# Decay and phase sums of a gated recurrence per chunk, in 64-row tiles of TensorE

## The chip, the cores and the metric

One Trainium2 chip, one core. The metric is the device time of one execution in microseconds; shown are the median and the range of the runs. PE is TensorE, DVE is VectorE, ACT is ScalarE, POOL is GpSimd, SP is SyncE.

## What is computed

A linear recurrence with a complex decay over 768 steps, for 4 batches of 8 heads of width 48, and then a layer norm and a two-layer network with a residual. Cut to what matters:

```python
mag = sqrt(a_re**2 + a_im**2); scale = minimum(mag, 0.999) / (mag + 1e-6)
ar, ai = a_re * scale, a_im * scale
for t in range(768):
    S_re, S_im = ar[t] * S_re - ai[t] * S_im + outer(k[t], v[t]), ar[t] * S_im + ai[t] * S_re
    y[t] = q[t] @ S_re
x = y with the heads side by side            # 4 x 768 x 384
xn = (x - mean) / sqrt(var + 1e-6) * g_ln
out = x + maximum(xn @ w_ch1, 0) @ w_ch2     # 384 -> 1536 -> 384
```

## The kernel before, in words

Time is cut into chunks of 128 steps, and two neighbouring chunks make a pair (P = 0 to 11, three for each batch; C = 128, R = 2). The recurrence is computed in the usual chunked way. For each pair the logarithm of the decay's magnitude (tile `l`) and its angle (`th`) are worked out, and both are summed over time. With `e = exp(sum)` and `en = exp(-sum)`, `ke = k * en` and `qe = q * e`; with cosine and sine of the summed angle (`trig`) these become `ks` and `qs`, in which the cosine and the sine part of a head lie side by side (48 of 64 columns each). Within a chunk n, scores `am` = ksT and qsT multiplied, masked into `atm`, times v; from earlier chunks comes the state `G`, times qsT. The sum of both is `y`, copied to `x`.

The tiles `l` and `th` hold two time steps in each of 128 partitions: partition p has steps 2p and 2p + 1 of the pair. So chunk 0 of a pair lies in partitions 0 to 63, chunk 1 in 64 to 127. The sum over time is done by TensorE: for each chunk c and step j a matmul with a matrix of zeros and ones (`u_e`, and `u_th` scaled to turns), four matmuls of 384 columns for the decay (`dec`, line 477) and four for the phase (`ph`, line 496). The kernel before sums over the whole pair: chunk 1 sees all 128 partitions. Two more matmuls of each phase sum (line 492) add, through the matrix `pick`, a constant and the phase carried over from the pair before (tile `car`, rows 96 to 127). `car` is copied out of the phase sum's bank after each pair (lines 504 to 512), the phase being read as a 16-bit integer, which takes it modulo one turn.

The state is kept relative to the start of a pair. For chunk 0 the products `ks` times v are added to the old state, which an identity matmul brings into the bank (line 641), and the result is copied to `G` without scaling. Chunk 1's products are added in the same bank, and there the state is scaled by the decay of the whole pair (`G`, line 658). That decay is the last row of `e`, turned onto partitions by eight one-column matmuls (`dps`, line 573) and copied into `dec` (`decc`, line 583).

Then each chunk's x is transposed (`xtr`, `xT`), and the network runs on the pair: `mm1` (line 722), `relu`, `mm2` (line 754), and `ot`, which applies the norm's scale and adds x. The norm's gain and mean are folded into the first weights (`wp`, `wc`).

The order of the work is written out by hand as a plan: a text of tokens `name:engine` with the PSUM bank, and each engine takes its tokens in that order. A token with `@other` waits in addition for that other operation. DMA issues are tokens too: most on SP, some on ACT, the weights on POOL. `warm` tokens are matmuls without use, 256 columns wide, that fill PE at the start. Pair 0 is split into two halves of four heads (`PARTS`), and its two chunks share a bank.

Of the kernel before, what the change touches and what calls it, by code (L numbers as in the profile page):

```python
# [9 lines left out]
FP32 = mybir.dt.float32  # L10
# [29 lines left out]
aim.0.0:A tab.log.0:A aim.0.1:A ue:G are.0.0:S are.0.1:S pad.e.1:G uth:V one:G warm.0:P0 pad.ks.0:G warm.1:P0  # L40
warm.2:P0 pick:G warm.3:P0 are.1.0:S warm.4:P0 warm.5:P0 warm.6:P0 k.0.1:S ln.0.0:A warm.7:P0 car0.1:G warm.8:P0
cmean:G iv.0.0:A warm.9:P0 ident:G warm.10:P0 warm.11:P0 r.0.0:V warm.12:P0 warm.13:P0 warm.14:P0 aim.1.0:S warm.15:P0
warm.16:P0 warm.17:P0 ln.0.1:A warm.18:P0 warm.19:P0 r2.0.0:A warm.20:P0 k.0.0:S warm.21:P0 warm.22:P0 warm.23:P0
warm.24:P0 u.0.0:A warm.25:P0 warm.26:P0 warm.27:P0 warm.28:P0 iv.0.1:A warm.29:P0 l.0.0:V warm.30:P0 are.2.0:S
# [12 lines left out]
warm.110:P2 warm.111:P2 warm.112:P2 qe.1.0.0:V warm.113:P2 warm.114:P2 pad.qs.1:G warm.115:P2 warm.116:P2 l.2.0:V
th.0.0:A warm.117:P2 warm.118:P2 wl.2:G warm.119:P2 ph.0.0:P1 th.0.1:A th.1.0:A qe.0.0.0:V ph.0.1:P4 qe.0.1.0:V
warm.120:P0 warm.121:P0 warm.122:P0 k.1.0:S car.0.0:V1 decc.0:V5 sin.0.0:A1 lc.2.0:V sin.0.1:A4 qt.0.0:P1 ks.0.0.1:V
warm.123:P0 car.0.1:A4 wgc:V cos.0.0:A1 qt.0.1:P4 ph.1.0:P6 k.1.1:S ks.0.1.1:V cos.0.1:A4 qs.0.1.1:V th.2.0:A  # L60
qs.0.0.1:V qs.0.1.0:V wp.1:P5 ks.0.1.0:V sin.1.0:A6 qs.0.0.0:V ks.0.0.0:V qT.1:P4 wc.1.2:V5 tab.log.2:A qT.0:P1
qsT.1:V4 kT.1:P0 qs.1.0.1:G@wc.1.2 dec.2.0:P2 car.1.0:V6 ln.3.0:A warm.124:P4 qsT.0:V1 warm.125:P4 wp.0:P4 e.2.0:A2
are.4.0:S wc.1.0:V5 kT.0:P1 en.2.0:A2 vf.1.0:S ksT.1:V0 ksT.0:A1 wc.0.0:V4 vf.1.1:S am.1:P2 warm.126:P0 wc.1.1:V5
iv.3.0:A warm.127:P0 am.0:P0 wc.0.2:V4 qt.1.0:P6 tab.trig.3:A warm.128:P5 warm.129:P5 warm.130:P5 warm.131:P5
wc.0.1:V4 warm.132:P5 warm.133:P5 atm.0:V0 ph.2.0:P4 r.3.0:G@wc.0.1 cos.1.0:A6 k.2.0:S v.0:A wp.2:P6 atm.1:V2
aim.4.0:S sin.2.0:A4 gm.0:P7 ke.1.0.0:G y.0:P0 G.0:V7 k.2.1:S x.0:A0 qt.2.0:P4 ke.1.0.1:V gm.1:P7 cos.2.0:A4 y.1:P1
q.2.0:S qs.1.0.0:V xtr.0:P0 ks.1.0.0:V x.1:A1 qT.2:P3 th.3.0:A ks.1.0.1:V qT.3:P5 qsT.2:V3 xtr.1:P1 q.2.1:S xT.0:A0
r2.3.0:G@ks.1.0.1 kT.3:P4 qsT.3:A5 xT.1:V1 kT.2:P2 ksT.3:V4 mm1.0.0.0:P0 G.1:V7 q.3.1:S tab.log.4:A v.1:G am.3:P4
ksT.2:V2 mm1.0.0.1:P0 are.5.0:S ke.2.0.0:G atm.3:V4 ln.4.0:A mm1.0.1.0:P2 q.3.0:S wl.3:G mm1.0.1.1:P2 relu.0.0:A0
wc.2.0:V6 am.2:P4 wc.2.2:V6 relu.0.1:A2 gm.2:P7 k.3.0:S atm.2:V4 ph.3.0:P0 qe.2.0.0:G@wc.2.2 G.2:A7 k.3.1:S iv.4.0:A  # L70
y.3:P2 wl.4:G wc.2.1:V6 y.2:P3 x.3:A2 gm.3:P7 pad.ks.2:G u.3.0:A mm1.0.2.0:P4 x.2:V3 r.4.0:G@wc.2.1 bn.3:V xtr.2:P6
xtr.3:P3 mm1.0.2.1:P4 xT.2:A6 xT.3:V3 G.3:V7 tab.trig.5:A mm1.1.1.0:P2 relu.0.2:V4 qe.2.0.1:G are.6.0:S mm1.1.1.1:P2
sin.3.0:A0 wl.5:G mm1.1.2.1:P6 bn.0:V vf.2.0:S relu.1.1:A2 mm1.1.0.1:P4 pad.qs.2:G l.3.0:V mm1.1.2.0:P6 abs.3.0:A0
r2.4.0:V mm1.1.0.0:P4 th.4.0:A car.3.0:V0 mm2.0.0:P2 relu.1.0:A4 ke.2.0.1:V mm2.1.0:P3 qs.2.0.1:V vf.2.1:S cos.3.0:A
lc.3.0:V mm2.2.0:P4 qs.2.0.0:V bn.2:V tab.log.6:A qT.4:P5 mm2.1.1:P3 bn.1:V rstd.1:G dec.3.0:P0 ks.2.0.1:V u.4.0:A
ks.2.0.0:V mm2.0.1:P2 rstd.0:G en.3.0:A0 l.4.0:V ksT.5:S mm2.2.1:P4 e.3.0:A0 lc.4.0:V ln.5.0:A relu.1.2:V6
qe.3.0.1:G@lc.4.0 mm2.1.2:P3 qe.3.0.0:G mm2.0.2:P2 aim.5.0:S oa.1:A3 qT.5:P0 iv.5.0:A vf.3.0:A ot.0:V2 dec.4.0:P6
qsT.4:V5 mm2.2.2:P4 e.4.0:A6 vf.3.1:A qs.3.0.1:V kT.4:P1 qs.3.0.0:V en.4.0:A6 dps.3:P5 are.7.0:S dps.4:P2 ksT.4:V1
ke.3.0.0:G@qs.3.0.0 qT.6:P3 qsT.5:A0 ph.4.0:P6 ot.2:V4 aim.6.0:S ke.3.0.1:G ln.6.0:A decc.3:V5 decc.4:V2 am.4:P4
q.4.0:S v.2:G qsT.6:V3 mm2.3.0:P1 iv.6.0:A atm.4:V4 ks.3.0.1:G k.4.0:S qT.7:P2 tab.trig.7:A mm2.3.1:P1 qsT.7:V2  # L80
gm.4:P3 am.5:P4 sin.4.0:A6 ks.3.0.0:V k.4.1:S y.4:P2 atm.5:V4 r.5.0:G@ks.3.0.0 kT.6:P0 car.4.0:A6 mm2.3.2:P1 x.4:A2
G.4:A3 ksT.6:V0 k.5.1:S kT.7:P5 abs.4.0:A6 xtr.4:P4 ot.1:G y.5:P0 ksT.7:V5 q.4.1:S th.5.0:A am.6:P6 x.5:V0 v.3:G
k.5.0:S am.7:P2 xT.4:A4 atm.6:V6 xtr.5:P0 ph.5.0:P4 r2.5.0:G xT.5:A0 cos.4.0:A ot.3:V1 gm.6:P0 mm1.2.1.1:P6 atm.7:V2
G.6:A0 vf.4.1:A r.6.0:G aim.7.0:S abs.5.0:A4 y.6:P1 mm1.2.1.0:P6 x.6:V1 sin.5.0:A4 vf.4.0:A mm1.2.2.1:P2 relu.2.1:V6
cos.5.0:A xtr.6:P1 r2.6.0:G y.7:P4 mm1.2.2.0:P2 th.6.0:A st.0:A x.7:V4 gm.7:P0 bn.7:V xtr.7:P4 tab.log.8:A ke.4.0.1:G
mm1.2.0.0:P6 xT.6:V1 mm1.2.0.1:P6 q.5.1:S xT.7:V4 qe.4.0.0:G G.7:V0 u.5.0:A are.8.0:S mm1.3.0.1:P4 bn.6:V ke.4.0.0:G
# [3 lines left out]
q.6.0:S r.7.0:V mm2.4.0:P1 e.5.0:A4 qT.8:P7 q.7.0:S bn.5:V v.4:A r2.7.0:G@r.7.0 dec.6.0:P4 are.9.0:S bn.4:V  # L90
relu.3.2:A2 mm2.4.1:P1 k.6.0:S qsT.8:V7 mm2.6.1:P0 rstd.2:G en.6.0:A4 qe.5.0.1:V am.8:P2 ke.5.0.0:V e.6.0:A4
mm2.4.2:P1 qe.5.0.0:V ln.8.0:A atm.8:V2 gm.8:P7 ke.5.0.1:G@qe.5.0.0 q.6.1:S am.9:P4 iv.8.0:A mm2.6.2:P0 qe.6.0.0:G
atm.9:V4 u.7.0:A st.1:A mm2.5.2:P6 ph.6.0:P2 G.8:A7 vf.6.0:A ks.5.0.1:V k.6.1:S tab.trig.9:A qs.5.0.1:V mm2.7.0:P4
ot.4:V1 abs.6.0:V2 y.8:P5 th.7.0:A vf.5.1:A mm2.7.1:P4 l.7.0:V x.8:A5 vf.5.0:A gm.9:P7 y.9:P1 sin.6.0:A2 vf.6.1:A
# [119 lines left out]
def kernel(  # L214
# [115 lines left out]
    def c_pick():  # L330
        nc.gpsimd.memset(pick, 0.0)
# [492 lines left out]
```

## Time and profile before

| | |
|---|---|
| median of 3 runs | 191.35 us (191.23 to 193.47) |
| profiled execution | 192.75 us, its span 191.0 us |
| PE busy | 177.3 us (93%) |
| VectorE, ScalarE busy | 156.6 us (82%), 158.9 us (83%) |
| GpSimd busy | 105.5 us (55%) |
| DMA | 37.57 MB, 197 GB/s in the mean |

The page's busy times are sums over the whole span. A stage that is limited by loads and one that is limited by PE are mixed in them, so busy time is also read by stretches. A line of a grouped view gives: line, engine, operation, output and input by the program's names, shapes and count, then busy time, the mean duration of one in ns, and the idle time before with what ended it. A line of the chain of waits or of the timeline starts with the start and the duration in us.

### The profile page before, as it was taken

How to read it: one execution, taken by the hardware profiler on the slowest of the kernel's cores; microseconds unless marked ns; L12 is line 12 of the kernel's file. 1: busy time of each engine (PE TensorE's matmuls, PEld its weight loads, DVE VectorE, ACT ScalarE, POOL GpSimd, SP SyncE). 2: the span in 40 equal slices, each digit the busy share in tenths (PEclk: the TensorE clock that was granted, in tenths of full speed). 3: DMA queues.
4: the chain of work that ended last, by engine and by line, in shares of the span. 5: the costliest groups of instructions: out<-in, count | busy, mean ns of one | idle time of the engine just before them, and what ended most of it. 6: DMA issues, size and time to landing. Idle time of an engine off the chain costs nothing.

```text
span 191.0 us, 5154 instructions
## 1 busy us (share of the span) xinstructions
PE 177.3 (93%) x2045; PEld 138.6 (73%) x2045; DVE 156.6 (82%) x285; ACT 158.9 (83%) x224; POOL 105.5 (55%) x124
## 2 busy tenths in 40 slices
PE   5999398999999999999968999999999999998992
PEld 3888365788667887776847687877867777786781
DVE  1678699999999999999996998998989867666532
ACT  3989499999999997899949999998999979662340
POOL 7419032579196899071539483347785954940130
PEclk9999999999999999999999999999999999999998
DMA  6999999999969999889999999999799979994032
GB/s 153 278 240 202 212 198 204 210 214 207 242 108 287 205 220 234 154 183 234 136 265 234 190 221 230 282 223 204 141 160 262 217 126 179 256 191 151 5 124 82
DMA packets 133080, 37.57 MB, mean 197 GB/s; under 512 B 127168, under 2 KB 133056, under 8 KB 133056
## 3 DMA queue, kind: packets, MB, share of 16 engines
q1 hardware_dynamic: 107760, 27.21, 70.6%
q10 hardware_dynamic: 22512, 7.67, 18.0%
q0 software_dynamic: 2784, 2.36, 7.9%
q8 instruction: 16, 0.26, 0.6%
q14 instruction: 8, 0.07, 0.1%
HBM read 28.31 MB, written 4.72 MB: 173 GB/s over the span
## 4 chain that ended last, share of the span: by engine, by line
PE 63%; DVE 10%; ACT 9%; DMA 8%; issue 4%; ACTq 2%; POOL 1%; SPq 1%; DVEq 0%; POOLq 0%
PE banks L754 22%; PE banks L722 16%; PE banks L617 5%; PE banks L594 4%; DMA q<-in_q_dram 4%; DMA ksT<-ks 3%; PE banks L477 3%; PE banks L667 2%; ACTq L777 2%; PE banks L496 2%; PE banks L670 2%; DVE w1b L388 2%; DMA are<-in_a_re_dram 2%; PE banks L645 2%; PE banks L688 2%
## 5 line engine op out<-in xcount | busy, mean ns | idle before, releaser
L754 PE MATMUL banks<-w2b,h 128*128 128x384 bf16 (+1 forms) x300 | 55.7, 319 | 0.6 <-ACT h L739 0.6
L722 PE MATMUL banks<-xT,w1b 128*128 128x256 bf16 x432 | 50.9, 272 | 0.7 <-ACT h L739 0.5
L722 PEld LDWEIGHTS <-w1b 128*128 128x128 bf16 x432 | 41.4, 98 | 7.0 <-issue 1.2
L754 PEld LDWEIGHTS <-h 128*128 128x128 bf16 x300 | 26.7, 97 | 13.8 <-ACT h L739 1.0
L295 DVE TENSOR_TENSOR atm<-banks,mask 128x1024 bf16<-128x1024 f32 x24 | 29.0, 1219 | 3.8 <-PE banks L617 2.9
L739 ACT ACTIVATE h<-banks 128x1024 bf16<-128x1024 f32 (+1 forms) x26 | 25.7, 1009 | 4.6 <-DVE ks L295 2.6
L792 ACT ACT_TABLE_LOAD x19 | 24.4, 1283 | 2.6 <-PEq L808 1.3
L295 POOL TENSOR_TENSOR ke<-k,en 128x384 bf16<-128x384 f32 x17 | 15.4, 916 | 14.1 <-ACT e L481 4.3
L767 POOL TENSOR_TENSOR ot<-ot,x 128x384 f32<-128x384 f32 x13 | 12.5, 967 | 14.2 <-ACT ot L760 12.9
L295 POOL TENSOR_TENSOR r<-aim,are 128x768 f16<-128x768 f32 (+1 forms) x8 | 13.7, 1715 | 11.0 <-DVE w1b L388 4.1
L787 PE MATMUL banks<-u_e 128*128 128x256 f16 x134 | 17.5, 286 | 2.2 <-POOL u_e L323 2.2
L295 POOL TENSOR_TENSOR qs<-qe,trig 128x768 bf16<-128x768 bf16 x8 | 13.0, 1640 | 10.3 <-DVE w1b L388 7.2
L617 PE MATMUL banks<-qsT,ksT 128*128 128x128 bf16 x192 | 14.5, 219 | 2.8 <-ACT h L739 2.1
L787 PEld LDWEIGHTS <-u_e 128*128 128x128 f16 x134 | 13.5, 102 | 4.5 <-POOL u_e L323 1.9
L617 PEld LDWEIGHTS <-ksT 128*128 128x128 bf16 x192 | 12.1, 97 | 5.1 <-issue 2.8
L741 DVE TENSOR_SCALAR h<-banks 128x1024 bf16<-128x1024 f32 (+1 forms) x11 | 12.7, 1166 | 2.7 <-PE banks L722 2.7
L295 POOL TENSOR_TENSOR qe<-q,e 128x384 bf16<-128x384 f32 x12 | 11.0, 917 | 6.8 <-DVE r L295 3.6
L466 DVE SCALAR_TENSOR_TENSOR l<-r,w 128x768 f16<-128x768 f16 (+1 forms) x13 | 12.6, 969 | 1.3 <-ACT r L462 1.1
L680 DVE BATCH_NORM_STATS2 stats<-x 128x6 f32<-128x384 bf16 x24 | 13.1, 546 | 0.1
L667 PE MATMUL banks<-v,atm 128*128 128x48 bf16 x192 | 12.0, 183 | 0.0
L514 ACT ACTIVATE trig<-banks 128x768 bf16<-128x768 int16 (+1 forms) x13 | 9.8, 761 | 2.5 <-DVE car L509 2.4
L496 PE MATMUL banks<-th,u_th 128*128 128x384 f16 (+1 forms) x52 | 11.8, 313 | 0.0
(93 smaller groups left out, 380.8 us busy)
## 6 DMA issues: line engine op xcount, KB each, us to landing
k<-in_k_dram SPq DMA_DIRECT2D x24, 192.0 KB, 5.1
q<-in_q_dram SPq DMA_DIRECT2D x24, 192.0 KB, 4.3
are<-in_a_re_dram SPq DMA_DIRECT2D x11, 384.0 KB, 5.1
aim<-in_a_im_dram SPq DMA_DIRECT2D x11, 384.0 KB, 5.0
out_dram<-ot ACTq DMA_DIRECT2D x19, 192.0 KB, 3.4
vf<-in_v_dram ACTq DMA_DIRECT2D x18, 192.0 KB, 4.3
w1b<-in_moe_w_ch_dram POOLq DMA_DIRECT2D x3, 384.0 KB, 7.6
vf<-in_v_dram SPq DMA_DIRECT2D x6, 192.0 KB, 7.0
```

The lines of the kernel that those rows point to most:

```text
L295: {"DVE": nc.vector, "POOL": nc.gpsimd}[eng(name)].tensor_tensor(**kw)
L466: nc.vector.scalar_tensor_tensor(out=S_("l"), in0=S_("r2"), scalar=0.5, in1=S_("w"), op0=ALU.mult, op1=ALU.add)
L496: nc.tensor.matmul(heads(ps[:, c]), lhsT=u_th[:, c, j], rhs=step(T("th", P), j), start=False, stop=(j == R - 1), skip_group_check=True)
L617: nc.tensor.matmul(ps[:, h], lhsT=T("ksT", n)[:, h], rhs=T("qsT", n)[:, h], start=True, stop=True)
L667: nc.tensor.matmul(ps[:, h], lhsT=T("atm", n)[:, h], rhs=T("v", P)[:, c, h], start=True, stop=nfirst)
L680: nc.vector.bn_stats(out=T("stats", n), in_=T("x", n))
L722: nc.tensor.matmul(ps[:, jj], lhsT=w1b[:, dc, ts(gi * JG + jj, C)], rhs=T("xT", P)[:, dc].rearrange("p c t -> p (c t)"), start=(dc == 0), ...
L739: act(out=dst, in_=src, func=AF.Relu)
L741: nc.vector.tensor_scalar(out=dst, in0=src, scalar1=0.0, scalar2=None, op0=ALU.max)
L754: nc.tensor.matmul(bank(own)[:, 0:w], lhsT=T("h", P)[:, j, ts(c, C)], rhs=w2b[:, j, es], start=(j == 0), stop=(j == NJ - 1))
L787: g.add(f"warm.{i}", lambda i=i: nc.tensor.matmul(bank(f"warm.{i}")[:, 0:256], lhsT=u_e[:, 0, 0], rhs=u_e[:, 1].rearrange("p j t -> p (j t ...
L792: g.add(f"tab.{nm}.{i}", lambda tab=tab: nc.scalar.preload_act_table_set(tab))
```

## The change

- Decay sums: for pairs 1 to 11 the matmul of chunk c takes only the rows of its chunk (64 partitions) of `u_e` and of `l`, in the order c = 0, c = 1 for each j. Pair 0 keeps full rows, with the part of `u_e` that joins chunk 1 to chunk 0 set to zero.
- Phase sums: the same for pairs 1 to 11. The carry is added to chunk 0 by one matmul with 64 rows. A new step `car1` copies the phase at the end of chunk 0 to rows 96 to 127 of `car`, and a new matmul `ph2` adds it to chunk 1. The carry to the next pair now lies in rows 32 to 63. Sine, cosine, absolute value and carry wait for `ph2`.
- State: scaled after each chunk, on VectorE. The identity matmul stands in every chunk but the first of a batch, behind the products. `dps` takes the last rows of both chunks, and also runs for the last pair of a batch.
- The plan is another one: other order, other engines for a part of the copies, products and DMA issues, 52 tokens with `@` where there were 27, and 64 fill-ins of 512 columns where there were 134 of 256.

```diff
-        for row in (HALF, C - 1):
+        nc.gpsimd.tensor_copy(out=pick, in_=pick_f)
+        for row in (HALF - 1, C - 1):
...
+    def c_pickf():
+        nc.vector.memset(pick_f, 0.0)
+        for c in range(R):
+            nc.vector.memset(pick_f[ds(c * HALF, 1)], 1.0)
+    def c_uz():
+        nc.vector.memset(u_e[0:HALF, 1], 0.0)
...
-                for c in range(R):
-                    for j in range(R):
-                        nc.tensor.matmul(heads(ps[:, c]), lhsT=u_e[:, c, j], rhs=step(T("l", P), j),
-                                         start=(j == 0), stop=(j == R - 1))
+                for j in range(R):
+                    for c in range(R):
+                        rows = ds(c * HALF, HALF) if NS == 1 else slice(0, C)
+                        nc.tensor.matmul(heads(ps[:, c]), lhsT=u_e[rows, c, j],
+                                         rhs=step(T("l", P), j)[rows],
+                                         start=(j == 0 and (NS == 1 or c == 0)), stop=(j == R - 1),
+                                         skip_group_check=True)
...
+                if NS == 1:
+                    for j in range(R):
+                        for c in range(R):
+                            rows = ds(c * HALF, HALF)
+                            nc.tensor.matmul(heads(ps[:, c]), lhsT=u_th[rows, c, j],
+                                             rhs=step(T("th", P), j)[rows], start=(j == 0),
+                                             stop=False, skip_group_check=True)
+                    nc.tensor.matmul(ps[:, 0], lhsT=(pick_f if first else pick)[lo],
+                                     rhs=T("car", P)[lo, fs], start=False, stop=True,
+                                     skip_group_check=True)
+                    return
...
+                add(f"car1.{X}", lambda X=X, fs=fs, v16=v16: f_car(
+                    f"car1.{X}", T("car", P)[96:C, fs], v16()[96:C, 0]),
+                    needs=[f"ph.{X}", f"car0.{P % RINGS['car']}"], uses=[("car", P)], ps=(f"ph.{X}", nb))
+                add(full, lambda X=X, fs=fs, view=view: nc.tensor.matmul(
+                    view(f"ph.{X}")[:, 1], lhsT=pick[HALF:C], rhs=T("car", P)[HALF:C, fs],
+                    start=False, stop=True, skip_group_check=True),
+                    needs=[f"ph.{X}", f"car1.{X}", "pick"], uses=[("car", P)], ps=(f"ph.{X}", nb))
...
-                needs=[f"ph.{X}"], uses=[("trig", P)], ps=(f"ph.{X}", nb))
+                needs=[full], uses=[("trig", P)], ps=(f"ph.{X}", nb))
...
+        ncol = H if last else R * H
+            for i in range(ncol):
+                nc.tensor.matmul(bank(f"dps.{P}")[:, ds(i, 1)], lhsT=row[:, ds(i * D, C)],
+                                 rhs=ident[:, C - 1:C], start=True, stop=True)
...
+                    for h in range(H):
+                        nc.tensor.matmul(heads(ps)[:, h], lhsT=T("ks", P)[:, c, h],
+                                         rhs=T("v", P)[:, c, h], start=(h == 0), stop=nfirst,
+                                         skip_group_check=True)
+                    if not nfirst:
                         nc.tensor.matmul(ps, lhsT=ident,
                                          rhs=T("G", n - 1).rearrange("p h d -> p (h d)"),
-                                         start=True, stop=True, skip_group_check=True)
+                                         start=False, stop=True, skip_group_check=True)
...
+                add(f"G.{n}", lambda n=n, c=c: tt(
+                    f"G.{n}", out=T("G", n), in0=heads(bank(f"gm.{n}")[:, 0:DM]),
+                    in1=T("dec", P)[:, c].unsqueeze(2).to_broadcast([C, H, D]), op=ALU.mult),
...
-    for i in range(134):
+    for i in range(64):
         g.add(f"warm.{i}", lambda i=i: nc.tensor.matmul(
-            bank(f"warm.{i}")[:, 0:256], lhsT=u_e[:, 0, 0], rhs=u_e[:, 1].rearrange(
-                "p j t -> p (j t)"), start=True, stop=True), needs=["ue"], ps=(f"warm.{i}", 1))
+            bank(f"warm.{i}"), lhsT=u_e[:, 0, 0], rhs=u_th.rearrange(
+                "p c j t -> p (c j t)"), start=True, stop=True), needs=["ue", "uth"], ps=(f"warm.{i}", 1))
```

More of the change, by code (lines that the diff above doesn't have):

```diff
@@ L39 @@
 PLAN = """
[L40 to L44, printed above, removed]
@@ L60 @@
[L60 to L64, printed above, removed]
@@ L70 @@
[L70 to L74, printed above, removed]
@@ L90 @@
[L90 to L94, printed above, removed]
@@ new lines @@
+v.4:G@r.7.0 ln.8.0:A dps.5:P4 decc.5:V4 mm2.6.1:P0 qsT.8:V7 dec.6.0:P4 qe.5.0.1:G en.6.0:A4 e.6.0:A4 iv.8.0:A
+ke.5.0.0:G@r.7.0 bn.5:V mm2.5.1:P6 bn.4:V am.8:P2 atm.8:V2 mm2.4.1:P1 vf.5.1:A am.9:P4 atm.9:V4 k.6.0:S are.9.0:S
+mm2.5.2:P6 ph.6.0:P2 car1.6.0:V2 rstd.3:A rstd.2:A qe.6.0.0:G@r.7.0 gm.8:P7 G.8:V7 u.7.0:A mm2.7.0:P4 ph2.6.0:P2
+qe.5.0.0:G@lc.6.0 ot.5:V6 qs.5.0.1:V vf.5.0:S vf.6.1:A tab.trig.9:A th.7.0:A sin.6.0:A2 l.7.0:V y.8:P5 y.9:P7
+aim.8.0:S x.9:A7 abs.6.0:V2 mm2.7.1:P4 aim.9.0:S mm2.7.2:P4 car.6.0:A2 qs.5.0.0:V mm2.4.2:P1 ot.1:G@qs.5.0.1 oa.7:A4
```

277 lines of the change are left out of this document (138 added, 139 removed).

## The prediction

> **What bounds the kernel now.** I read the page's head and chain first, then busy time by stretch.
>
> ```profile
> span 191.0 us, 5154 instructions
> PE 177.3 (93%) x2045; PEld 138.6 (73%) x2045; DVE 156.6 (82%) x285; ACT 158.9 (83%) x224; POOL 105.5 (55%) x124
> PE 63%; DVE 10%; ACT 9%; DMA 8%; issue 4%; ACTq 2%; POOL 1%; SPq 1%; DVEq 0%; POOLq 0%
> ...
> core 0: us, PE busy (x) PEld busy (x) DVE busy (x) ACT busy (x) POOL busy (x), PEclk, DMA share, GB/s
> 0.00:36.00 36.00, 29.64 (x298) 23.08 (x298) 26.64 (x51) 29.41 (x45) 15.77 (x37) 1.00 1.00 211
> 36.00:187.00 151.00, 147.44 (x1748) 115.50 (x1747) 129.00 (x234) 129.53 (x181) 89.71 (x87) 1.00 0.98 196
> 187.00:191.00 4.00, 0.21 (x3) 0.00 (x0) 0.92 (x3) 0.00 (x0) 0.00 (x0) 0.78 0.29 98
> ```
>
> Three stages. Until about 36 us the fill-in matmuls keep PE busy and loads and ScalarE set the pace. From 36 to 187 us PE is busy 147.44 of 151.00 us at full granted clock, with ScalarE and VectorE near 129, so in this stage a microsecond of matmul work is nearly a microsecond of time. The only slack to win back there is 151.00 - 147.44 = 3.56 us. The last 4 us are the final output and its store. The change reorders those too, but ends as before on a half-width output add and its store, so I give the end nothing.
>
> The profiled execution took 192.75 us for a span of 191.0 (1.75 around it); the three runs have a median of 191.35. I work out a difference and add it to the median. 2% of it, 3.8 us, is about what a measurement of this kernel can tell from no change.
>
> **What PE saves by 64-row tiles.** A matmul's mean is no price, as neighbours overlap; the price is the step from start to start.
>
> ```profile
> L477 PE MATMUL banks<-l,u_e 128*128 128x384 f16 x44 | 8.9, 326 | 0.0
> L641 PE MATMUL banks<-G,ident 128*128 128x384 bf16 x8 | 2.6, 326 | 0.0
> L594 PE MATMUL banks<-ident,ks 128*128 128x128 bf16 x80 | 5.9, 219 | 0.0
> L573 PE MATMUL banks<-ident,e 128*128 128x1 bf16 x64 | 2.5, 164 | 0.1
> ...
> 44.13 0.66 PE banks L722 x6
> 53.04 0.65 PE banks L477 x4
> 58.21 0.45 PE banks L594 x8
> 58.66 0.38 PE banks L573 x16
> ...
> 41.98 0.32 PE L492 MATMUL banks<-car,pick 96*128 96x384 f16 x1
> 42.15 0.49 PE L496 MATMUL banks<-th,u_th 128*128 128x384 f16 x2
> 42.47 0.33 PE L492 MATMUL banks<-car,pick 96*128 96x384 f16 x1
> 42.64 0.49 PE L496 MATMUL banks<-th,u_th 128*128 128x384 f16 x2
> 42.97 0.18 PE L667 MATMUL banks<-v,atm 128*128 128x48 bf16 x1
> ```
>
> Four decay matmuls hold the path for 0.65 us, so one 384-wide matmul costs 0.163; the six of a phase sum run from 41.98 to 42.97, again 0.163 each. The 326 ns mean is twice that: 0.163 of flow, and 0.163 of tail that normally hides under the next matmul.
>
> For eleven of the twelve pairs (pair 0, split in two, keeps whole-row tiles) the four decay matmuls become two couples, rows 0-63 and rows 64-127, in two banks. If a couple runs side by side, four steps become two: 11 x 2 x 0.163 = -3.58 us. The phase sum goes from six steps to two couples, one carry matmul and one more for chunk 1 ("ph2"), four in all: again 11 x 2 x 0.163 = -3.58. Together -7.2. If the halves don't run side by side, both savings are 0; no row of before has two row tiles, so -7.2 and 0 are the bounds. I take -7.2: the halves use different rows and banks, and nothing in the rows joins them.
>
> By the Trainium skill ("TensorE: Matmul & The Clock Gate", Part 3: Packing small matmuls) matmuls in different row groups run at once, starting some 4 ns apart; by that the couple is as cheap as I took it. No run here shows it yet.
>
> **What the tiles may cost.** The new order goes between 128-row and 64-row work 62 times (I counted the places where dec, ph or ph2 of pairs 1 to 11 meet another matmul). Let one change cost x. From below: the 96-row matmuls at 41.98 and 42.47, between 128-row neighbours, add nothing (0.17 and 0.32 to the next group), so x may be 0. From above: the whole tail is exposed, x = 0.163. So 0 to 10.1 us. The 96-row row is nearest, but it is no tile of half the array, while the tail is what a change of shape would have to wait for; I take the middle, 0.08: +5.0.
>
> The Trainium skill ("TensorEngine Tiling (Array Packing)", Tiling Modes, Key Properties) says that a change of the tiling mode, not of the tile alone, drains TensorE. By it x would be at the upper end, and the tiles would cost more than they save; that result is a rival below. The 96-row matmuls do not decide whether the trace agrees.
>
> **What PE gets in addition.** The state is scaled after every chunk: the identity matmul that carries it (L641) now stands in both chunks, 8 more, 8 x 0.163 = +1.3. The last row of the decay factors ("dps", L573) is taken for both chunks, and for the last pairs of a batch too: 8 x 8 + 4 x 8 = 96 more one-column matmuls at 0.38/16 = 0.024: +2.3 (a load of weights each, but those hide at 0.024 already). One group of eight transposes moves from DMA to PE: +0.45. Sum of PE: -7.2 + 5.0 + 1.3 + 2.3 + 0.45 = +1.9 (bounds -3.1, and +4.1 + 10.1 = +14 if nothing overlaps and each change drains).
>
> **The new wait.** The phase at the end of chunk 0 goes through a copy ("car1", ScalarE for seven pairs, VectorE for four) before ph2 may run, and sine, absolute value and the carry to the next pair now wait for ph2.
>
> ```profile
> L506 ACT ACTIVATE car<-banks 32x384 f16<-32x384 int16 x4 | 1.9, 483 | 0.1
> L509 DVE TENSOR_SCALAR car<-banks 32x384 f16<-32x384 int16 x3 | 1.7, 563 | 0.2
> L514 ACT ACTIVATE trig<-banks 128x768 bf16<-128x768 int16 x11 | 8.9, 811 | 0.1
> ```
>
> ph2 stands in PE's queue, so when it waits, the layer's matmuls, scores and outputs behind it wait, and then the engines that empty their banks. After ph: a tail of 0.16, on average half an instruction already running on the copying engine (0.4), the copy of 0.48 or 0.56, together about 1.1 us. The order puts PE work between ph and ph2 as cover: pair 5 has one half group of L722 (0.66), pair 3 two outputs (0.78), pair 9 about 2.1; the mean of eleven is about 1.15. So some are covered and some short; bounds 0 and, with a full instruction ahead each time (0.16 + 0.81 + 0.56 = 1.53, up to 0.9 short), about 0.5 x 11 = 5.5. I take 0.1 each: +1.0.
>
> **The start.**
>
> ```profile
> 7.60 2.12 DVE L469 TENSOR_SCALAR l<-l 128x384 f16<-128x384 f16 x1
> ...
> 4.20 0.52 ACT L448 ACTIVATE w<-are 128x384 f32<-128x384 f32 x1 [1.60 <-DMA are<-in_a_re_dram]
> 25.15 0.80 ACT L514 ACTIVATE trig<-banks 128x768 bf16<-128x768 int16 x1
> 40.55 1.92 ACT L739 ACTIVATE h<-banks 128x1024 bf16<-128x1024 f32 x2
> ...
> 38.10 0.82 PE L722 MATMUL banks<-xT,w1b 128*128 128x256 bf16 x6
> ```
>
> ScalarE runs from 4.20 us in its own order until it empties the first hidden group at 40.55. Laying its new list against the old one, from the sine of pair 1 (25.15) on, three items come in and three of like size go out: no change. On PE, though, the new order has less behind it at that first emptying: one transpose group (0.45), one score group (0.45) and two half groups of L722 (1.3) now stand after it: 2.2 us, the upper bound. The lower bound is -1: the cap at 7.60 took 2.12 us, and the new order has no GpSimd multiply beside it, but the second a_im half is now issued by ScalarE behind two activations. Nearer to the ScalarE list than to the full 2.2: +0.9. The fill-ins (134 narrow, now 64 twice as wide) only fill; they cost if they stand before something ready, 0.2 us at a time, inside that range.
>
> **The other engines.**
>
> ```profile
> L404 ACTq DMA_DIRECT2D vf<-in_v_dram x18: 374/401/641, 56.0 to 162.1; - x18
> L404 SPq DMA_DIRECT2D vf<-in_v_dram x6: 488/812/2875, 16.7 to 46.9; - x6
> L777 ACTq DMA_DIRECT2D out_dram<-ot x19: 338/363/2372, 70.4 to 173.6; - x19
> SPq L599 <- DVE ks L295: 14.3, 4, 6.6
> ...
> L295 DVE TENSOR_TENSOR G<-banks,dec 128x384 bf16<-128x384 f32 x8 | 4.4, 544 | 0.0
> L290 ACT CAST x<-banks 128x384 bf16<-128x384 f32 x12 | 5.7, 477 | 2.5 <-PE banks L670 2.5
> L295 POOL TENSOR_TENSOR ks<-ke,trig 128x768 bf16<-128x768 bf16 x5 | 8.2, 1639 | 5.3 <-DVE qs L295 5.1
> L295 DVE TENSOR_TENSOR ks<-ke,trig 128x768 bf16<-128x768 bf16 x17 | 9.0, 550 | 0.8 <-POOL ke L295 0.6
> ```
>
> ScalarE hands 17 DMA issues to SyncE (10 of v, 6 stores, 1 of a_im): 17 x 0.36 to 0.40 = 6.5 us of its queue. That can't return more than the 3.56 us of PE idle; I credit a third, -1.2 (0 to -3.56). SyncE's queue gains 16 issues of some 0.8, 13 us; it stood 14.3 us waiting for ks alone, so I price it at 0. If that room is gone, loads queued behind stores waiting for their results come late, and the q and k products with them.
>
> Eight state updates move from ScalarE to VectorE (8 x 0.544), eight casts of x the other way (8 x 0.477): even. Eleven ks and qs products move to GpSimd, where one takes 1.64 instead of 0.55: 11 x 1.09 = 12 us if all were waited for. They have most of a pair's layer matmuls as cover and GpSimd is at 55%: 0.
>
> **Sum.** PE +1.9, new wait +1.0, start +0.9, ScalarE relief -1.2: +2.6; with unrounded terms (-7.17 + 4.96 + 1.30 + 2.30 + 0.45 + 1.0 + 0.9 - 1.2) +2.54. 191.35 + 2.54 = **193.9 us**.
>
> **Rivals.**
>
> *Changing the tiles drains PE.* Place: the 62 changes. Without them the sum is -2.4, so the total is -2.4 + 62x, and it is slower by over 3.8 us once x passes 0.10. With the whole tail, 0.163: +7.7, 199.0 us. For it: the 0.163 of tail is there in each row; against it: the 96-row matmuls. Chance 0.21.
>
> *The halves run one after another*, so the tiles do not do what they say: no saving, no drain: -2.4 + 7.2 = +4.8, 196.1 us. For it: no row shows two at once. Chance 0.08.
>
> *The copy between the phase sums stops PE* at 0.5 us a pair: +2.54 - 1.0 + 5.5 = +7.0, 198.4 us. For it: ScalarE and VectorE are busy 129 of 151 us in the dense stage, so the copy seldom finds them free; against it: the order leaves a mean cover of 1.15. Chance 0.10.
>
> *The tiles are free and ScalarE's relief comes through.* x = 0, no new wait, an even start: -3.1, and 2.2 of the 3.56 us of idle regained: 186.0 us. For it: the 96-row matmuls, and ScalarE's 6.5 us; against it: PE's idle is small already. Chance 0.18.
>
> **How the numbers follow.** Forecast, within 2%: 0.43. Faster by over 2% (below 187.5): the last rival, 0.18. Slower (above 195.2): 0.21 + 0.08 + 0.10 = 0.39. The forecast's own range is 188.9 (x = 0) to 195. For 8 in 10 I go from 186.5, most of the way to the fast rival, to 200, past the drain's 199.0. Beyond lie a dry queue on SyncE or GpSimd above, and below an order that regains all idle.
>
> **What would show it.** Right: the decay group of a later pair steps 0.33 us plus a visible gap at both ends, PE's dense stage loses no matmul work in sum, PE waits for car1 at a few ph2, the first hidden group is emptied near 41 us. Wrong: gaps of 0.15 at every decay group, or 0.65 us for its four matmuls (rivals 1, 2); ph2 as the longest wait of PE (3); no gap at all, and PE's work 3 us less (4); or new waits on SyncE's loads or GpSimd's products, which I priced at nothing.

## The result, and the profile after

After takes 200.71 us (median of 4 runs, 199.92 to 201.48) beside 191.93 for before on the same chip: ratio 1.0523, interval 1.0473 to 1.0572. The forecast was 193.9, with a range up to 200. The change is 8.8 us slower, not 2.5. The ratio comes from fast executions alone and puts before at about 190.7 us (200.71 / 1.0523), so that by it the loss is about 10 us, and the profiled execution of before, 192.75 us, is one of the slow ones. The drain rival comes nearest (199.0), but by another cause.

The page of after, head and busy times:

```profile
span 198.9 us, 5261 instructions
PE 182.5 (92%) x2085; PEld 128.2 (64%) x2087; DVE 159.7 (80%) x286; ACT 159.3 (80%) x230; POOL 123.7 (62%) x137
```

PE is busy 5.2 us longer (177.3 before), GpSimd 18 us longer, VectorE 3 us and ScalarE the same. The stretches that matter are cut at the first layer matmul and at the ends of the layer matmuls of pairs 1, 3 and 11. First before, then after (columns as in the prediction's table of stretches):

```profile
0.00:38.10 38.10, 31.64 (x333) 25.06 (x334) 28.72 (x55) 31.51 (x48) 16.79 (x38) 1.00 1.00 212
38.10:49.60 11.50, 11.50 (x153) 10.04 (x151) 11.10 (x19) 11.20 (x15) 9.03 (x11) 1.00 1.15 217
49.60:78.50 28.90, 28.41 (x344) 22.13 (x342) 28.12 (x53) 26.93 (x36) 21.58 (x22) 1.00 0.96 205
78.50:183.20 104.70, 101.74 (x1189) 78.33 (x1187) 86.06 (x157) 88.69 (x126) 56.58 (x53) 1.00 0.99 193
183.20:191.00 7.80, 4.01 (x37) 3.01 (x35) 2.55 (x5) 0.61 (x2) 1.51 (x2) 0.89 0.29 102
```

```profile
0.00:38.65 38.65, 30.86 (x263) 16.42 (x266) 28.92 (x50) 32.54 (x50) 27.29 (x48) 1.00 1.04 217
38.65:52.70 14.05, 13.51 (x175) 11.25 (x175) 11.42 (x21) 13.06 (x16) 10.38 (x10) 1.00 1.12 208
52.70:85.10 32.40, 31.24 (x385) 22.90 (x383) 31.02 (x57) 27.70 (x41) 20.25 (x16) 1.00 0.81 178
85.10:191.40 106.30, 102.84 (x1233) 74.53 (x1232) 86.66 (x159) 85.09 (x123) 65.80 (x63) 1.00 0.91 186
191.40:198.90 7.50, 4.05 (x38) 3.05 (x36) 1.65 (x4) 0.89 (x3) 0.00 (x0) 1.00 0.15 54
```

The lengths of the five stretches differ by +0.55, +2.55, +3.5, +1.6 and -0.3. So of 7.9 us of span, 6.6 are lost by the end of pair 3 and only 1.6 in the eight pairs behind it. In the second stretch before had PE busy for all of its 11.50 us; after it is idle 0.54 and has 2.0 more work there.

What PE executes from 38.65 us on, from the groups of matmuls by shape:

```profile
L626 PE MATMUL banks<-ident,qs 128*128 128x128 bf16 x80 | 6.1, 219 | 0.0
L626 PE MATMUL banks<-ident,ks 128*128 128x128 bf16 x72 | 5.2, 219 | 0.6 <-DVE ks L292 0.6
L677 PE MATMUL banks<-G,ident 128*128 128x384 bf16 x15 | 4.8, 322 | 0.0
L506 PE MATMUL banks<-th,u_th 64*128 64x384 f16 x36 | 4.7, 327 | 0.0
L486 PE MATMUL banks<-l,u_e 64*128 64x384 f16 x36 | 4.5, 326 | 0.4 <-DVE l L477 0.2
L606 PE MATMUL banks<-ident,e 128*128 128x1 bf16 x120 | 4.3, 163 | 0.0
L536 PE MATMUL banks<-car,pick 64*128 64x384 f16 x9 | 3.0, 330 | 0.0
```

Before has 120 transposes, 8 identity matmuls, 48 one-column matmuls and 90 whole-row steps of decay and phase sums behind its first layer matmul (counted by their starts). After has 152, 15, 120, and 36 couples and 18 single steps. This cut at the first layer matmul is what the prediction's counts left out: x36 in L486 is nine pairs, not eleven, as the sums of pairs 1 and 2 run among the fill-ins.

A step is the time from the start of one matmul to the start of the next, and a gap is what a step has above the usual one of its shape. With them, the 7.70 us by which the stretch from the first layer matmul to the last matmul's start grew (148.86 to 156.56) come apart like this: 32 transposes more +1.78, identity +1.14, one-column +1.73, sums 36 steps fewer -5.87, 52 changes between 128 and 64 rows at 0.095 +4.94, gaps over 0.15 us +2.52 (5.08 to 7.60), shorter gaps +1.46 (what is left). So the 64-row tiles by themselves win 0.93 us here: 5.87 less the 4.94 of their changes.

The chain of waits of after shows a couple and a change:

```profile
86.64 0.67 PE banks L781 x4
87.32 0.43 PE banks L486 x4
87.75 0.76 PE banks L781 x4
88.50 0.45 PE banks L649 x8
```

L781 is the output matmul, four of which need 0.65. Between 86.64 and 88.50 lie two such groups and four decay matmuls: 1.86 us. Two couples at 0.163 would make 0.65 + 0.33 + 0.65 = 1.63; both changes together are 0.23, of which 0.095 on the way in and 0.092 on the way out recur at nearly every change of the trace. In most couples the second matmul starts 3 ns behind the first. PE's waits for other engines behind the first layer matmul, the three longest of before:

```profile
PE banks L617 <- ACT h L739: 2.1, 1, 2.1
PE banks L754 <- ACT h L739: 0.6, 1, 0.6
PE banks L722 <- ACT h L739: 0.5, 1, 0.5
```

Before waits for ScalarE's hidden groups (`h`) and little else. In after the waits are small and scattered; four of them:

```profile
PE banks L781 <- ACT h L766: 1.6, 1, 1.6
PE banks L626 <- DVE ks L292: 0.6, 2, 0.4
PE banks L749 <- DVE sh L565: 0.5, 1, 0.5
PE banks L673 <- POOL v L422: 0.4, 1, 0.4
```

No line of PE's waits names ph2 (L536).

### The profile page after: what moved, and what is told of

Its sections match the earlier page's. It is cut to its first block, busy times and chain, and to the rows that moved or that the text cites. A ratio compares the mean times of both kernels' runs of the same rounds, so it can differ in the third digit from the quotient of the medians.

```text
span 198.9 us, 5261 instructions
## 1 busy us (share of the span) xinstructions
PE 182.5 (92%) x2085; PEld 128.2 (64%) x2087; DVE 159.7 (80%) x286; ACT 159.3 (80%) x230; POOL 123.7 (62%) x137
## 4 chain that ended last, share of the span: by engine, by line
PE 50%; DVE 15%; ACT 11%; DMA 8%; issue 5%; SPq 5%; POOL 4%; ACTq 0%; POOLq 0%; DVEq 0%
PE banks L781 17%; PE banks L749 15%; SPq L412 5%; DMA q<-in_q_dram 4%; PE banks L649 3%; PE banks L626 2%; DMA aim<-in_a_im_dram 2%; PE banks L694 2%; ACT h L766 2%; DVE qsT L289 2%; PE banks L715 2%; DVE h L768 2%; DVE atm L292 2%; POOL r L292 1%; ACT L819 1%
## 5 line engine op out<-in xcount | busy, mean ns | idle before, releaser
L781 PE MATMUL banks<-w2b,h 128*128 128x384 bf16 (+1 forms) x300 | 56.2, 319 | 2.0 <-ACT h L766 1.6
L781 PEld LDWEIGHTS <-h 128*128 128x128 bf16 x300 | 25.9, 97 | 16.1 <-issue 3.2
L292 POOL TENSOR_TENSOR qs<-qe,trig 128x768 bf16<-128x768 bf16 (+1 forms) x13 | 21.1, 1625 | 18.0 <-PE banks L626 7.0
L292 POOL TENSOR_TENSOR ke<-k,en 128x384 bf16<-128x384 f32 x21 | 19.2, 920 | 10.2 <-ACT e L492 5.6
L814 PE MATMUL banks<-u_th,u_e 128*128 128x512 f16 x64 | 17.1, 403 | 3.4 <-DVE u_th L326 2.6
L292 POOL TENSOR_TENSOR ks<-ke,trig 128x768 bf16<-128x768 bf16 (+1 forms) x11 | 17.6, 1612 | 1.0 <-DVE ke L292 0.6
L292 POOL TENSOR_TENSOR r<-aim,are 128x768 f16<-128x768 f32 (+1 forms) x8 | 12.9, 1610 | 7.4 <-DVE ks L292 2.7
L768 DVE TENSOR_SCALAR h<-banks 128x1024 bf16<-128x1024 f32 (+1 forms) x12 | 14.1, 1178 | 2.5 <-PE banks L749 2.2
L474 DVE SCALAR_TENSOR_TENSOR l<-r,w 128x768 f16<-128x768 f16 (+1 forms) x13 | 11.6, 890 | 5.0 <-ACT r L470 4.8
L292 DVE TENSOR_TENSOR G<-banks,dec 128x384 bf16<-128x384 f32 x20 | 11.0, 548 | 4.7 <-PE banks L677 4.6
L794 POOL TENSOR_TENSOR ot<-ot,x 128x384 f32<-128x384 f32 x9 | 8.9, 986 | 8.1 <-ACT ot L787 5.4
L292 POOL TENSOR_TENSOR qe<-q,e 128x384 bf16<-128x384 f32 x14 | 12.7, 917 | 1.7 <-DMA q<-in_q_dram 1.0
L814 PEld LDWEIGHTS <-u_e 128*128 128x128 f16 x64 | 6.4, 103 | 10.4 <-issue 3.9
```

The source lines that it names most:

```text
L292: {"DVE": nc.vector, "POOL": nc.gpsimd}[eng(name)].tensor_tensor(**kw)
L474: nc.vector.scalar_tensor_tensor(out=S_("l"), in0=S_("r2"), scalar=0.5, in1=S_("w"), op0=ALU.mult, op1=ALU.add)
L768: nc.vector.tensor_scalar(out=dst, in0=src, scalar1=0.0, scalar2=None, op0=ALU.max)
L781: nc.tensor.matmul(bank(own)[:, 0:w], lhsT=T("h", P)[:, j, ts(c, C)], rhs=w2b[:, j, es], start=(j == 0), stop=(j == NJ - 1))
L814: g.add(f"warm.{i}", lambda i=i: nc.tensor.matmul(bank(f"warm.{i}"), lhsT=u_e[:, 0, 0], rhs=u_th.rearrange("p c j t -> p (c j t)"), start= ...
```

## The experiments

Behind each time stands its ratio to before on the same chip, with the interval. Gains and losses against after are differences of ratios, in us of 191, where nothing else is said.

**Order and sums apart.** The first keeps before's sums and takes after's order with its engines, and the identity in each chunk as that order has it; the second takes the new sums in before's order, with the new steps put in where they fit and all state updates on VectorE, as the change has them.

```diff
+ e1: before's code with after's plan, but for car1.*, ph2.*, dps.2, dps.5, dps.8, dps.11 and their decc;
+                    if not nfirst:
+                        nc.tensor.matmul(ps, lhsT=ident, ..., start=False, stop=True)
+     and 64 fill-ins of 512 columns
+ e2: after's code with before's plan, and in it car1.*, ph2.*, dps.2, dps.5, dps.8, dps.11 and their decc
```

> The new order with the sums of before: pair-wide decay and phase on whole rows, no copy between the chunks, state scaled once per pair; the identity matmul stays in both chunks (8 more, +1.3 us of PE). Theory A, the order costs: the starts of the matmuls after the change give the new sums about +2.8 us of PE, so about 6 of the 8.8 us are the order's, and this run comes at 191.9 + 6 + 1.3 = 199 us. Theory B, the sums cost (tile changes and the copy that is waited for): this run falls back to 192 to 194 us.

> The order of before with the sums of after: 64-row tiles, copy and second carry matmul, state scaled per chunk, last rows of both chunks; the new tokens are put in where the old order lets them, the second carry matmul after 0.45 to 1.1 us of other PE work. Theory A (order): 191.9 + 2.8 of PE + up to 11 x 0.2 of waits at the second carry matmul = 195 to 197 us. Theory B (sums): 199 to 201 us, as after.

e1 took 197.96 us beside 190.86: 1.037 (1.0324 to 1.0416), +7.1. The new order without the new sums costs seven tenths of the loss (0.037 of 0.0523), with the identities in it. Its trace has 32 transposes more behind the first layer matmul (+1.78), seven identities (+1.14) and 2.35 us more of gaps over 0.15. e2 took 208.91: 1.0937 (1.0866 to 1.1009), worse than either part of the change would give; its gaps over 0.15 us are 13.0 us, and its granted clock falls to 0.57 from 36 to 38 us and to 0.72 from 118 to 124, so a part of its time may be the clock's. Before's order doesn't fit the new sums, so e2 prices their meeting and not the sums. The difference of after and e1 does: 0.0153 of 191, 2.9 us for sums, copies and one-column matmuls together.

**The phase without its copy.**

```diff
-                            rows = ds(c * HALF, HALF)
-                            nc.tensor.matmul(heads(ps[:, c]), lhsT=u_th[rows, c, j],
...
+                rows = slice(0, 96) if first else slice(0, C)
+                for c in range(R):
+                    nc.tensor.matmul(ps[:, c], lhsT=pick[rows], rhs=T("car", P)[rows, fs],
...
-car1.1.0:V6 ph2.1.0:P6 car1.2.0:A4 ph2.2.0:P4 ...
```

> After, with one part undone: the phase sum is pair-wide on whole rows again, without the copy and the second carry matmul; decay tiles, state and order stay. PE work: 0.98 instead of 0.33 + 0.33 + 4 changes of 0.095 = 1.04 per pair, so -0.7 us. Theory C, the copy between the phase sums stops the queue: 3 to 5 us faster than after, 196 to 198. Theory A (order): within 1 us of after, 199.5 to 200.7.

199.57 us, 1.0444 (1.0397 to 1.049): 1.5 us less than after, with intervals that overlap. The copy doesn't stop PE by 3 to 5 us. That the chunk-wise phase is dearer than the whole one is likely, not shown.

**More changes of tile in before.**

```diff
-                rows = slice(0, 96) if first else slice(0, C)
+                rows = (slice(0, 96) if NS > 1 else slice(HALF, 96)) if first else slice(HALF, C)
```

> Before, with the two carry matmuls of each phase sum of pairs 1 to 11 cut to the rows that are not zero in the matrix: 64 to 127, and 64 to 95 in the first pair of a batch. The sums are the same; the only new thing is 4 changes between whole rows and fewer rows per pair, 44 in all. Theory D, each change costs PE the 0.095 us seen in after: +4.2 us, 196 us. If a change is free, as the 96-row matmuls of before are: 192 us.

194.26 us, 1.0152 (1.008 to 1.0225): +2.9. The carry matmuls now take 32 or 64 rows between whole-row ones, and the chain of waits of e4 shows both:

```profile
86.86 0.26 PE banks L492
87.13 0.43 PE banks L496 x2
87.56 0.26 PE banks L492
87.82 0.43 PE banks L496 x2
```

0.26 and 0.43 stand where 96-row matmuls had 0.17 and 0.32 (rows at 41.98 and 42.15 of before): a change to 64 rows costs 0.1 each way, one to 96 rows nothing. The 36 changes behind the first layer matmul make 3.5 us by their steps; 2.9 were measured, and the interval holds both.

By the Trainium skill ("TensorEngine Tiling (Array Packing)", Tiling Modes, Key Properties) a change of tiling mode drains TensorE. The trace agrees in part: each change to 64 rows has a price, but 0.095 and not the whole tail of 0.163, and the 96-row rows show none.

**One cause of the order at a time, in after.** Pair 1's q loads earlier on SyncE; 15 ks and qs products back from GpSimd; 19 v loads and stores back to ScalarE; the first two stores later.

```diff
+ e5: q.1.0:S q.1.1:S earlier in the plan
+ e6: ks.0.1.0:V qs.0.1.0:V ... ks.11.0.1:V   (15 tokens, :G in after)
+ e7: st.2:A vf.4.0:A st.0:A vf.5.0:A ...     (19 tokens, :S in after)
+ e9: st.2:S st.0:S later in the plan
```

> After, with one part of the order changed: on SyncE the two q loads of pair 1 are issued right after the second k load of pair 0, ahead of the second v load and both k loads of pair 1. In after GpSimd's q product of pair 1 waits for the second of them until 28.9 us, and pair 0's layer matmuls end 2.6 us later than before the change. If that load is what the start loses to: 1 to 2 us faster than after, 198.7 to 199.7 against 200.7. If another thing follows right behind it (ScalarE's list, the k products now late): within 0.7 us of after.

> After, with the 15 ks and qs products that the change moved from VectorE to GpSimd put back on VectorE at the same place in the order. Theory F, GpSimd's 1.64 us products make the transposes and the state late: 2 to 4 us faster than after, 197 to 199. If VectorE is as short as GpSimd in the stages that count (15 x 0.55 = 8 us more for it): no gain, 200 to 203.

> After, with the 19 v loads and stores that the change moved from ScalarE to SyncE issued by ScalarE again, at the same place in the order (the last four stores stay as after has them). Theory G, loads on SyncE stand behind stores that wait for results, and the DMA engines run dry (56 to 71 us): 2 to 3 us faster than after, 198. If it doesn't matter: 200.7 to 202, as ScalarE gets 19 x 0.37 = 7 us of issues back.

> After, with only the first two stores moved on SyncE's queue: they stand behind the loads of pairs 4 to 7 instead of ahead of them. In after SyncE waits 6.5 us for the first of them, up to 64.4. Theory G: 1 to 2 us faster than after, 199. If the load behind it (the decay input of pair 8, which waits for its buffer until 70.7) holds the queue anyway: within 0.7 us of after.

201.12 (1.053, 1.0447 to 1.0614), 209.51 (1.0962, 1.0882 to 1.1042), 207.79 (1.0856, 1.0769 to 1.0942) and 200.76 us (1.0482, 1.0411 to 1.0552). By the medians two do nothing and two make it 7 to 9 us worse. Putting work back on its old engine in a new order is no undoing: in e6 GpSimd waits 12.9 us at once for `en`. So e5 and e9 rule out their two places as causes that could be taken out alone, and e6 and e7 rule nothing out.

**The start and the carry.**

```diff
+ e10: ks.1.0.0:V ks.1.0.1:V right behind qs.1.0.0:V; ke.1.0.1:G ahead of r.3.0:G; kT.3, kT.2 ahead of mm1.0.0.1
+ e11: car.3.0:V0 behind abs.3.0:A0, ahead of sin.3.0:A0
+ e12: both
```

> The kernel after, with the products of pair 1 taken out of GpSimd's row of work: both ks products of pair 1 run on VectorE right behind qs.1.0.0 and ahead of the state G.1, ke.1.0.1 stands ahead of r.3.0 on GpSimd, and the key transposes of pair 1 stand ahead of the first layer matmul. Theory A (the order's price begins with GpSimd's row at the start, where pair 1's last ks ends at 39.5 us and not at 36.9): the end of pair 0's layer matmuls comes about 1 us earlier than after's, and most of that is kept to the end: 198.7 to 200.0 us against after's 200.7. Theory B (the start is absorbed later, and the whole is set by how far the other engines lag from 48 us on): pair 0 ends earlier and pair 3 where it did, 200.3 to 201.2 us.

> The kernel after, with the copy of the carry car.3.0 right behind abs.3.0, ahead of the sine that reads the same bank. Theory A (VectorE's 1.7 us of waiting at 49.8 us, behind that sine, is what makes its chain from 51 to 69 us late, and with it pairs 2 and 3): pair 2 ends 1 to 1.5 us earlier than after's, 199.2 to 199.9 us. Theory B (VectorE's chain has room there; the layer matmuls wait for GpSimd's products and for loads): no change, 200.3 to 201.1 us.

> The two edits together: products of pair 1 on VectorE, and the carry ahead of the sine. If the order's price lies at these two places: 197.2 to 198.7 us. If it is spread over many places that each have a little less cover: 199.8 to 201 us.

202.32 (1.0655, 1.0543 to 1.0768), 200.81 (1.0588, 1.0473 to 1.0704) and 201.24 us (1.062, 1.0487 to 1.0754): no gain that shows in time. The trace of e11 is worth reading. VectorE waits 1.70 us in after behind a sine that reads the same bank, and then works without a break:

```profile
51.53 0.56 DVE L528 TENSOR_SCALAR car<-banks 32x384 f16<-32x384 int16 x1 [1.70 <-ACT trig L546]
52.12 0.96 DVE L474 SCALAR_TENSOR_TENSOR l<-r,w 128x768 f16<-128x768 f16 x1
```

In e11 the copy comes first, and the logarithm 1.7 us sooner:

```profile
47.72 0.56 DVE L527 TENSOR_SCALAR car<-banks 32x384 f16<-32x384 int16 x1 [0.21 <-ACT sh L562]
49.32 1.21 DVE L767 TENSOR_SCALAR h<-banks 128x1024 bf16<-128x1024 f32 x1
50.45 0.94 DVE L473 SCALAR_TENSOR_TENSOR l<-r,w 128x768 f16<-128x768 f16 x1
```

The stretch between the ends of pair 1's and pair 2's layer matmuls shrinks from 26.05 to 24.76 us, as it should if that chain holds it up. But `h`, which stood at 48.61, now stands at 49.32, and pair 1's layer matmuls take 5.36 us instead of 4.44. The gain is paid for in the pair before. In e10 16 transposes are back ahead of the first layer matmul, and that matmul comes at 39.55 instead of 38.65.

**Handing DMA issues to SyncE, alone, in before.**

```diff
+ e8: vf.4.0:A st.0:A st.2:A vf.6.0:A ...  ->  :S, each at its old place (19)
```

> The kernel before, with 19 loads of v and stores of outputs handed from ScalarE's queue to SyncE's, each at its old place in the order; nothing else is changed. It tests a step of the prediction by itself: 16 more issues on SyncE at no cost, and a relief of 1.2 us on ScalarE. If that step is right: 190.2 to 191.9 us against before's 191.9. If loads behind stores in SyncE's queue come late, with the products that need them: 193.5 us and more, and new waits of VectorE or GpSimd on loads of q and k.

191.36 beside 191.74 us: 1.0003 (0.9949 to 1.0058). In before's order SyncE's issues are free, as priced, and ScalarE's relief of 19 issues brings nothing that shows: the interval ends at -1.0 us, short of the -1.2.

**Load off one engine, moved to none.** The half width leaves out half of the products, hidden values or masked scores.

```diff
+ e13 (after), e16 (before):
+                        if P >= 4 and eng(f"{nm}.{X}.{a}") == "POOL":
+                            hw, fw = slice(0, H // 2), slice(0, DM // 2)
+ e14 (after), e17 (before):
+                    if P >= 4 and not end and eng(name) == "ACT":
+                        dst, src = T("h", P)[:, ds(gi * JG, JG // 2)], src[:, 0:JG // 2]
+ e19 (after):
+                js = slice(0, DM if P in (3, 4) else None)
+                    nh = H // 2 if 4 <= n < 8 else H
```

> The kernel after, with GpSimd's 15 ks and qs products of pairs 4 to 11 at half their columns (the other half of ks and qs keeps old values): about 12 us of GpSimd work less, in the same order. Theory A (the 11 more products on GpSimd, priced at nothing, are what the waits come from): 2 us and more are gained, about 198 us against after's 200.7. Theory B (ScalarE is the engine that PE waits for): under 1 us. Theory C (PE has more work, and its waits come from the places in the order and from no engine's load): under 1 us here and with ScalarE relieved.

> The kernel after, with ScalarE's 16 emptyings of hidden groups of pairs 4 to 11 at half their columns (the other half of h keeps old values): about 7 us of ScalarE work less, and each hidden group 0.45 us sooner free. Theory B (ScalarE): 2 us and more are gained, 198.5 us or less. Theory A (GpSimd) and theory C (places in the order): under 1 us, 199.9 to 201 us.

> The same half width of GpSimd's ks and qs products in the kernel before, 11 of them (9 us less work), as a control: before's order gives GpSimd more room, so all theories expect under 0.7 us gained (191 to 192 us). If it gains as much as the kernel after does, GpSimd is no part of the difference between the two.

> The same half width of ScalarE's emptyings of hidden groups in the kernel before, 17 of them, as a control. PE's waits there are for ScalarE's hidden groups (3.2 us of 3.4 us): up to 2 us gained, 189.5 to 191.5 us. If it gains as much as the kernel after does, ScalarE is no part of the difference between the two.

> The kernel after, with VectorE's masking of the scores of chunks 4 to 7 and its decay logarithms (l) of pairs 3 and 4 at half their columns (the other half keeps old values): 3.4 us of VectorE work less between 52 and 73 us. Theory A (VectorE's unbroken row of work from 51.5 us on makes PE's waits of pairs 2 and 3): about 1 us of the 1.70 us of waits ahead of pair 2's layer matmuls goes, pair 2 ends 0.7 to 1.3 us earlier, 199.4 to 200.1 us. Theory B (they come from GpSimd or from loads): no change in that stretch, 200.4 to 201 us.

GpSimd: 200.42 us, 1.047 (1.0408 to 1.0533) in after and 190.29, 0.9973 (0.9924 to 1.0021) in before: 12 us less of its work in after is worth about 1 us by the ratios and 0.5 by the stretch from first layer matmul to last matmul. In before 9 us less are worth 0.5 by the ratio and 1.9 by that stretch. So GpSimd's larger load from pair 4 on is at most a small part of the cause. ScalarE: 198.77, 1.0393 (1.0325 to 1.046) and 190.64, 0.995 (0.991 to 0.999): 2.5 us in after, 1 in before; from first layer matmul to last matmul 1.8 and 1.4 us. ScalarE holds PE in both orders, and 0.4 (by the stretches) to 1.5 us (by the ratios) of the difference may be its own.

VectorE, early: 199.42 us, 1.0466 (1.0406 to 1.0525). In after, then in e19, the stretch from pair 1's to pair 2's layer matmuls:

```profile
52.70:78.75 26.05, 24.91 (x329) 18.02 (x327) 24.84 (x47) 21.39 (x34) 18.36 (x16) 1.00 0.79 178
```

```profile
52.70:77.85 25.15, 24.82 (x329) 18.33 (x327) 22.09 (x46) 21.42 (x34) 18.40 (x16) 1.00 0.82 186
```

PE's work is the same (24.91, 24.82), VectorE's 2.75 us less, and the stretch 0.9 us shorter. By the steps the gaps over 0.15 us go from 1.70 to 0.72. So PE waits here for VectorE's unbroken row behind its late start at 51.53, for about 1 us; this is the one place of waits in after that is shown. That it is a part of the difference is not: the same load was not taken off in before, whose VectorE is as dense between the ends of pairs 1 and 3 (28.12 of 28.90 us, beside 31.02 of 32.40).

**The start undone.**

```diff
- after's plan up to the first layer matmul
+ before's plan and engines up to it, with car1 and ph2 of pairs 1 and 2 added; then what is left, in after's order
```

> The kernel after with its start undone: everything that before's order has ahead of the first layer matmul is taken in before's order and on before's engines (with the new copies car1 and second phase matmuls ph2 of pairs 1 and 2 put in), and all that is left follows in after's order. Theory A (the start's order is a main part of the price): the first layer matmul is 0.5 to 1.9 us earlier than after's 38.65, all 64 early transposes again stand ahead of it (24 more than in after, 1.3 us of PE work), pair 0's layer matmuls end 2 to 3 us earlier, and 197.5 to 198.7 us are measured. Theory B (what the start loses is absorbed later, by the other engines' chains): under 1 us gained, 199.7 to 201 us.

203.63 us, 1.0676 (1.0615 to 1.0736): worse. All 64 early transposes stand ahead of the first layer matmul again and pair 0's stretch is 0.6 us shorter, but that matmul comes at 39.87 us, and PE's gaps up to pair 2 grow from 2.6 to 4.7 us. In e2, nearly the same start with the old order behind it, it came at 40.93. The 2 us that were expected can't be had by putting one start before another's middle.

## Why the prediction was wrong

**Right.** The couples run side by side (3 ns apart), so the halves-one-after-another rival is out. A change costs 0.095 where 0.08 was taken, and lies just below the 0.10 from which it would decide. That the changes come to +4.94 for +4.96 is luck: 52 of them count and not 62, each dearer than was taken. The identity (+1.14 for +1.30) and the one-column matmuls (+1.73 for +2.30) are as priced, less what runs in the start. The copy doesn't stop PE: no wait names ph2, and e3 bounds it; +1.0 was too much. SyncE's issues are free in before's order (e8), and GpSimd's products have cover, at least from pair 4 on (e13). ScalarE empties the first hidden group at 41.40 us, where "near 41" was said.

**Wrong, first step: the other engines.** "I credit a third, -1.2" and the moves called even were the largest miss. Nothing of PE's idle came back; gaps grew by 2.5 us over 0.15 and by 1.5 below. With the +1.0 for the copy and the -1.2, -0.2 was forecast and +4.0 measured: 4.2 of the 5.4 us between the forecast's difference (+2.5) and the spans' (+7.9). The reason that it was credited was a sum of queue time, 6.5 us; e8 shows that the same relief by itself is worth nothing that shows, and at most 1.0 us. What the order does to latencies was costed at nothing, though it is another order in every pair. That the order costs is shown by e1, where it stands without the new sums. Where in the order is shown for a small part: of these 4 us, about 1 may be VectorE's chain at 51 us (e19, e11) and up to 1.5 ScalarE's load (e14, e17). For the others no single place is shown; e5, e9, e10 and e11 exclude the loads of q, the two stores, pair 1's products and the carry as causes that could be taken out alone.

**Wrong, second step: PE's sum.** It was made for the whole kernel, though the text itself says that up to 36 us fill-ins keep PE busy. The savings of pairs 1 and 2 (and their changes) fall there and count nothing: -5.87 for -7.17. And three groups of transposes, besides the one counted, moved from ahead of the first layer matmul to behind it: +1.34, of which the 2.2 us given for the start saw only what delays ScalarE's first emptying. PE's part without gaps is +3.7, not +1.84.

**The start.** +0.9 was given, +0.55 found against the profile of before. That profile's start was late itself: with the same start untouched, e4, e16 and e17 had the first layer matmul at 37.09, 36.74 and 36.97 us. Against these it is +1.6 to +1.9, inside the bound. The gaps of that profile are large too: e4, in before's order, has 2.95 us over 0.15, where the profile of before has 5.08. So what is added up here from the spans (+7.9) is rather low, which fits the medians (+8.8) and the ratio (about +10).

**The range** ended at the dearest single rival. Here the price x of a change was near the middle of its bounds, and the other engines, PE's sum and the start were all dearer at once; the range had no case for that.

**Open.** Why the first layer matmul comes at 38.4 to 40.9 us in every profile with the new order or the new sums, and at 36.7 to 38.1 in four of five with before's (41.4 in e8). The two latest have a lower granted clock ahead of it: e2 (40.93 us) 0.57 from 36 to 38 us, e8 0.50 from 24 to 28; e15 (39.87) has not. Open too are some 2 to 3 us of gaps without an owner.

## What to carry to other kernels

Add up only what stands behind the point where the bounding engine becomes dense: here work saved among fill-ins counted for nothing, and work moved across that point for its full price. When a whole order is replaced, price the order as a part of its own, with the first pairs step by step, and credit no queue relief that no wait in the profile names. Undoing one token of such an order tells little; taking load off one engine without moving it told more, where the kernel before was run as a control.

## What the runs showed of the hardware

A 64-row matmul among 128-row ones costs 0.095 us going in and 0.092 to 0.103 coming out (after and e4; in e4 a 32-row one the same); a 96-row one costs 0.00 (before). Two 64-row matmuls on different rows start 3 ns apart in most couples of after.

Some VectorE operations take several times as long beside GpSimd's. From the timelines of after, first VectorE (start, duration), then GpSimd:

```profile
15.24 3.82 DVE L383 TENSOR_SCALAR gc<-cmean,gln 128x128 bf16<-128x128 f32 x3
34.87 2.09 DVE L292 TENSOR_TENSOR qs<-qe,trig 128x768 bf16<-128x768 bf16 x1
```

```profile
16.69 1.79 POOL L292 TENSOR_TENSOR qe<-q,e 128x384 bf16<-128x384 f32 x2
35.60 0.93 POOL L292 TENSOR_TENSOR ke<-k,en 128x384 bf16<-128x384 f32 x1
```

The same two in before:

```profile
23.30 0.67 DVE L375 TENSOR_SCALAR gc<-cmean,gln 128x128 bf16<-128x128 f32 x3
35.46 0.55 DVE L295 TENSOR_TENSOR qs<-qe,trig 128x768 bf16<-128x768 bf16 x1
```

0.67 and 0.55 us became 3.82 and 2.09. In after each ends close behind GpSimd's own: 19.06 behind 18.48, 36.96 behind 36.53. VectorE operations that read a bank kept their time: `x` at 33.88 and `G` at 34.35 took 0.55 us each beside GpSimd's `r` from 33.00 to 34.81. In e10 GpSimd stands idle from 35.05 to 36.61 us, and the same product takes 0.56 us again:

```profile
34.98 0.56 DVE L291 TENSOR_TENSOR qs<-qe,trig 128x768 bf16<-128x768 bf16 x1
36.61 1.81 POOL L291 TENSOR_TENSOR r<-aim,are 128x768 f16<-128x768 f32 x1 [1.56 <-issue]
```

The first layer matmul of e10 came no sooner for it (39.55 us), so this alone doesn't make the start late. The Trainium skill ("SBUF — State Buffer", Who interferes with whom) says that a VectorE instruction with two inputs in SBUF contends with a GpSimd instruction that reads SBUF, over a pair of ports that the two engines share. The rows of `qs` fit that.
